# Chunk 0 halted after eight of w_out's rows, in unsplit float32 till there, and batches 6 and 7's state @ w_in made in eight float32 tiles in the pair phase

## The chip, the cores and the metric

The kernel runs on one core of a Trainium2 chip. The time is the device time of one execution in microseconds (us); less is better. TensorE (PE) multiplies, with its weight loads shown apart (PEld), VectorE (DVE) and ScalarE (ACT) work on tiles, GpSimd (POOL) does little here, and SyncE (SP) issues nearly all the transfers (DMA). Each engine works through a queue of its own in a fixed order.

## The reference

```python
def _attn_ref(x, state):                      # x: 8, 8, 512, 64   state: 8, 8, 32, 64
    scores = scale * np.matmul(x, state.transpose(0, 1, 3, 2))
    ...                                       # softmax over the 32 slots: a
    xread = np.matmul(a, state)
    scores2 = scale * np.matmul(state, x.transpose(0, 1, 3, 2))
    ...                                       # softmax over the 512 tokens: a2
    sread = np.matmul(a2, x)
    return np.concatenate([xread, sread], axis=2)

def _moe_ref(x, w_in, w_out):                 # x: 4608 tokens x 512, w_in: 512 x 2048, w_out: 2048 x 512
    h = x @ w_in
    g = h - np.tanh(h)
    return g @ w_out
```

## The kernel before

**Work.** Each of eight batches (chunk 0 to 7, 512 tokens each) never forms its xread: since xread is a @ state, its hidden layer is a @ (state @ w_in), so the kernel first makes m = state @ w_in (256 x 2048 a batch) and multiplies by a. The `sread` rows of all batches are a ninth chunk of 256 tokens at the end. Of each chunk, `hidden(f)` makes 128 of the 2048 hidden columns (f = 0 to 15) and `output(f)` multiplies them by rows 128 f to 128 f + 127 of w_out, "row f" below, and adds them up in four PSUM banks, one for each 128 tokens.

**Precision.** TensorE takes float32 operands in two ways here. A plain float32 matmul is two records in the trace. Or both operands are split in two float32r parts, high and low (`split`: ScalarE casts, VectorE subtracts), and three float32r matmuls do the work (high by high, high by low, low by high; lines 483 to 485 in `hidden`, 530 to 532 in `add`). Before the change only the first four `hidden` of chunk 0 are plain (`mlo is None`, line 481, and line 687 of the start-up); every `add` is split.

**Weights.** w_in and w_out come in as float64. Each row or tile is loaded as 512 KB and made float32 by three VectorE instructions and one ScalarE instruction (`Weight.steps`); w_out's rows are then split (`convert_wout`, tiles `wo`), and w_in's tiles go back to DRAM as float32 (`wf`) and are multiplied with the state.

**state @ w_in.** For batches 0 and 1 `m_first_two` does it while w_in is converted: eight plain matmuls of 64 x 32 weights by 512 columns, on eight parts of the array, for each pair of tiles. For batches 2 to 7 `m_units` does it later, in sixteen units: w_in is read back and split, six matmuls (line 232) make batches 2 to 5's part, three (line 239, tile `mls`) batches 6 and 7's. The results go to DRAM (`mdram`) and come back as `mr` when a chunk needs them.

**Order.** Chunks 0 to 3 are written as steps `st = 16 * i + f`. A step converts weights (`D0["conv"]`, `D0["wo"]`), writes `hidden` two steps ahead (`LAG`), then a piece of other work from tables (`ASIDE`: attention of later batches `att2` and so on, `m_units` as `m0`), then `output(f)`. Chunks 4 to 7 are done in two pairs by `Pair`, in ticks, with fewer products (sums and differences of w_out's rows, made by `mix_rows`, stand for some of them); attention of batches 6 and 7 lies in the first pair (`SIDES`). The scheduler sorts what is written into the five queues.

Of the kernel before, what the change touches and what calls it, by code (L numbers as in the profile page):

```python
# [19 lines left out]
P = 128  # L20
# [10 lines left out]
LONE = 1  # L31
TURN = (0, 1, 3, 2)
# [3 lines left out]
def attention_ffn(ctx: ExitStack, tc: tile.TileContext, xT, xn, bd, bh, sp, sm, sl, win, wout, xout, tout, sout):  # L36
# [24 lines left out]
    AB = int('2')  # L61
# [17 lines left out]
        if b >= 2  # L79
        else None  # L80
        for b in range(B)
    ]
    wf = [dram.tile([P, 4, 512], F32, name=f"wf{q}") for q in range(NQ)]
# [70 lines left out]
    def second(q):  # L154
        if q < 2:
            return pool.tile([P, 2, 512], F32, tag="stage", name=f"mr1{q}", bufs=SB)
        return pool.tile([P, 2, 512], F32, tag="g", name=f"mr1{q}", bufs=GB)

    def m_first_two(q, p):

        k = p // 2
        if p == 0:

            m_first[q] = pool.tile([P, 2, 512], F32, tag="mr", name=f"mr0{q}", bufs=RRB)
            m_second[q] = second(q)
        if p % 2 == 0:
            return
        pss = [bank(ps_a, f"mps0{q}{p - 1 + c}") for c in range(2)]
        run = []
        for b in range(2):  # L170
            for c in (1, 0):
                for e in range(2):
# [3 lines left out]
                    with ExitStack() as behind:  # L176
                        if run:
                            behind.enter_context(tc.issue_after(run[-1]))
                            behind.enter_context(tc.high_priority())
                        made = nc.tensor.matmul(  # L180
                            pss[c][rows], sps[r, p - 1 + c, rows], wfs[q, k][r, c], start=True, stop=True
                        )
                    if not run:
                        behind_free(made)
                    run.append(made.ins)
        for c in range(2):
# [18 lines left out]
    def m_units():  # L205
# [4 lines left out]
        raw = pool.tile([P, 4, P], F32, tag="stage", name="slr", bufs=SB)  # L210
        s1 = parts("sls", [P, 2, 4, P], F32R)
        nc.sync.dma_start(raw, sl)
        split(s1[:, 0], s1[:, 1], raw)
        for q in range(NQ):
            for k in range(2):
                w = pool.tile([P, 2, 512], F32, tag="wf", name=f"w1{q}{k}", bufs=WB)
                nc.sync.dma_start(w, wf[q][:, 2 * k : 2 * k + 2])
                for c in range(2):
# [4 lines left out]
                    ps2 = bank(ps_h, f"mls{q}{p}")  # L223
# [14 lines left out]
                    for n, (x, y) in enumerate(((0, 0), (0, 1), (1, 0))):  # L238
                        nc.tensor.matmul(ps2, s1[:, x, p], t[:, y], start=(n == 0), stop=(n == 2))  # L239
                    late = pool.tile([P, 512], F32, tag="c2", name=f"sl{q}{p}", bufs=CSB)  # L240
                    nc.scalar.copy(late, ps2)
                    stage = pool.tile([P, 2, 512], F32, tag="stage", name=f"st{q}{p}", bufs=SB)
                    for e in range(2):
                        free(stage[:, e], pss[e])
# [3 lines left out]
                    for e in range(2):  # L248
                        for j in range(2):
                            rows = slice(64 * e + 32 * j, 64 * e + 32 * j + 32)  # L250
                            nc.sync.dma_start(mdram[6 + j][q][k, 2 * c + e], late[rows])
                    yield

    def load_m(b, q):
        if b < 2:
            r = (m_first, m_second)[b][q]
# [25 lines left out]
    def convert_wout(f, part):  # L282
        w = pool.tile([P, 512], F32, tag="c2", name=f"wor{f}", bufs=CSB)
        part.convert(w)
        wo[f] = big(f"wo{f}", [P, 2, DM], F32R)
        split(wo[f][:, 0], wo[f][:, 1], w)


    def attention(b, aT):
# [22 lines left out]
        def all_scores():  # L312
# [3 lines left out]
            for j in (2, 0, 3, 1):  # L316
                at = TURN[j] if b < 2 else j
# [63 lines left out]
    def state_read(b, ss):  # L381
# [40 lines left out]
        for hf in range(2):  # L422
            for k in range(4):
                for c in range(4):
                    cs = slice(32 * c, 32 * c + 32)
                    j = TURN[c] if b < 2 else c
# [12 lines left out]
        for hf in range(2):  # L439
            for j in range(4):  # L440
                h = 4 * hf + (TURN[j] if b < 2 else j)
# [8 lines left out]
    def turn_sread():  # L450
        srT = pool.tile([P, 2, 4, 256], F32R, tag="aT", name="srT", bufs=AB)
# [9 lines left out]
    class Chunk:  # L461
        def __init__(self, i):
# [3 lines left out]
            self.g = {}  # L466

# [22 lines left out]
        def finish(self, f, ps):  # L490
            i, n = self.i, self.n
            t = pool.tile([P, 512], F32, tag="t", name=f"t{i}_{f}", bufs=TB)[:, :n]
            if CL <= i < B:
# [4 lines left out]
                return  # L498
            tanhs.append((nc.scalar.activation(t, ps, AF.Tanh).ins, nc.vector.tensor_sub(t, ps, t).ins))  # L499
# [4 lines left out]
        def output(self, f):  # L504
            n = self.n // P
            if f == 0:
                self.o = [bank(ps_o, f"ops{self.i}_{t}") for t in range(n)]
# [14 lines left out]
            if f == NFF - 1:  # L522
                for t in range(n):
                    self.store(t)

        def add(self, f, t):
            g, o = self.g[f], self.o[t]
            tok = slice(t * P, t * P + P)
            w = wo[f]
            nc.tensor.matmul(o, g[:, 0, tok], w[:, 0], start=(f == 0), stop=False)  # L530
            nc.tensor.matmul(o, g[:, 0, tok], w[:, 1], start=False, stop=False)  # L531
            return nc.tensor.matmul(o, g[:, 1, tok], w[:, 0], start=False, stop=(f == NFF - 1)).ins  # L532

        def store(self, t):
            i, o = self.i, self.o[t]
            ob = pool.tile([P, DM], F32, tag="ob", name=f"ob{i}_{t}", bufs=OB)
# [41 lines left out]
    def convert_win(q, p):  # L578
# [24 lines left out]
    aTs[0] = pool.tile([P, 2, 2, 512], F32R, tag="aT", name="aT0", bufs=AB)  # L603
# [26 lines left out]
    def step(op):  # L630
# [29 lines left out]
        elif k == "A":  # L660
            ats[j] = pool.tile([P, 512], F32, tag="ob", name=f"at0{j}", bufs=OB)
# [26 lines left out]
        elif k == "X":  # L688
            t = hts[j] = pool.tile([P, 512], F32, tag="t", name=f"t0_{j}", bufs=TB)
            a = nc.scalar.activation(t, hps[j], AF.Tanh)  # L690
            d = nc.vector.tensor_sub(t, hps[j], t)
# [3 lines left out]
        elif k == "G":  # L695
# [413 lines left out]
```

## Time and profile before

| | |
|---|---|
| Median of 3 runs | 664.64 us (663.02 to 666.04) |
| The profiled execution: its time, its span | 662.42 us, 660.6 us |
| Mean granted TensorE clock | 0.992 |
| Busy in the span: PE, PEld, DVE, ACT, POOL | 96%, 75%, 73%, 59%, 4% |
| Chain that ended last: PE, DVE, DMA, issue, ACT | 77%, 14%, 4%, 3%, 2% |
| HBM traffic | 93.91 MB read, 42.47 MB written |

Busy time on PE is modelled to each matmul's end, and matmuls overlap; on other engines it is the time of their instructions. A granted clock of 1.00 is 2.4 GHz, 0.50 is 1.2 GHz, and a value between is a stretch with both.

### The profile page before, as it was taken

The page shows a single profiled execution, that of the slowest core. Times are in us where ns is not written, and L with a number is a line of the kernel's source. Part 1 is how long each engine was busy: PE and PEld are TensorE (multiplying, and loading weights), DVE is VectorE, ACT ScalarE, POOL GpSimd, SP SyncE. Part 2 cuts the span into 40 slices and gives each one's busy share as a digit, 9 for nine tenths or more (in the row PEclk, how much of TensorE's full clock was granted, in tenths as well). Part 3 has the DMA queues.
Part 4 walks back from the last instruction along what each step waited for, and adds up shares of the span by engine and source line. Part 5 has one row for each costly group of instructions (what it writes and reads, how often), then busy time and mean ns, then how long its engine had stood idle before and what let it go on. Part 6 is the DMA issues. An engine that isn't in the chain of part 4 may idle for free.

```text
span 660.6 us, 9657 instructions
## 1 busy us (share of the span) xinstructions
PE 633.5 (96%) x3482; PEld 494.4 (75%) x3482; DVE 483.8 (73%) x769; ACT 389.2 (59%) x675; POOL 27.3 (4%) x41
## 2 busy tenths in 40 slices
PE   5879989999999999999999999999999999999997
PEld 2546667677777778787878887778888888788996
DVE  5999999639457876799637886996965789754442
ACT  3768875657667666576645576355655553543532
POOL 2000000000000000000000000000000000343300
PEclk9799999999999999999999999999999999999999
DMA  9799798356787974656722436464566535899800
GB/s 314 213 357 321 268 368 275 138 185 177 223 265 223 301 221 160 193 168 220 257 97 96 143 128 209 159 197 128 160 189 190 159 128 174 291 320 356 270 23 32
DMA packets 65199, 137.01 MB, mean 207 GB/s; under 512 B 6784, under 2 KB 28544, under 8 KB 65152
## 3 DMA queue, kind: packets, MB, share of 16 engines
q1 hardware_dynamic: 62592, 128.02, 59.5%
q0 software_dynamic: 2560, 8.39, 3.7%
q8 instruction: 27, 0.44, 0.3%
q14 instruction: 20, 0.16, 0.1%
HBM read 93.91 MB, written 42.47 MB: 206 GB/s over the span
## 4 chain that ended last, share of the span: by engine, by line
PE 77%; DVE 14%; DMA 4%; issue 3%; ACT 2%; SPq 0%; ACTq 0%; DVEq 0%
PE X L944 12%; PE hps L483 9%; PE hps L484 8%; PE hps L485 8%; PE ops L532 8%; PE ops L531 8%; PE ops L530 8%; PE Y1m L944 5%; PE Y0m L944 4%; PE mps L232 2%; PE mls L239 2%; PE rps L431 1%; DVE m L101 1%; DMA wo3d<-in_wout 1%; DVE w L131 1%
## 5 line engine op out<-in xcount | busy, mean ns | idle before, releaser
L531 PE MATMUL ops<-wo,g 128*128 128x512 f32 x256 | 99.9, 394 | 6.0 <-DVE wo L101 6.0
L483 PE MATMUL hps<-aT,m 128*128 128x512 f32 x248 | 99.3, 402 | 3.3 <-DVE G L497 1.3
L484 PE MATMUL hps<-aT,m 128*128 128x512 f32 x248 | 97.0, 391 | 0.0
L485 PE MATMUL hps<-aT,m 128*128 128x512 f32 x248 | 96.3, 391 | 0.0
L530 PE MATMUL ops<-wo,g 128*128 128x512 f32 x256 | 94.1, 396 | 0.9 <-ACT wo L101 0.8
L532 PE MATMUL ops<-wo,g 128*128 128x512 f32 x256 | 90.5, 394 | 0.0
L499 DVE TENSOR_TENSOR t<-hps,t 128x512 f32<-128x512 f32 (+1 forms) x78 | 49.5, 634 | 51.6 <-ACT t L499 51.3
L497 ACT ACTIVATE t<-hps 128x512 f32<-128x512 f32 x64 | 38.3, 599 | 61.8 <-PE hps L485 59.5
L497 DVE TENSOR_TENSOR G<-hps,t 128x512 f32<-128x512 f32 x64 | 43.9, 688 | 36.9 <-ACT t L497 36.9
L499 ACT ACTIVATE t<-hps 128x512 f32<-128x512 f32 (+1 forms) x78 | 43.3, 555 | 44.9 <-PE hps L485 42.3
L101 ACT CAST g<-t 128x512 fp32r<-128x512 f32 (+1 forms) x78 | 44.8, 579 | 32.0 <-DVE t L499 31.8
L483 PEld LDWEIGHTS hps<-aT,m 128*128 128x128 f32 x248 | 46.4, 188 | 22.9 <-ACT m L101 3.6
L531 PEld LDWEIGHTS ops<-wo,g 128*128 128x128 f32 x256 | 48.2, 188 | 19.0 <-DVE wo L101 8.3
L101 DVE TENSOR_TENSOR g<-t,g 128x512 fp32r<-128x512 f32 (+1 forms) x78 | 49.2, 633 | 14.8 <-ACT g L101 14.4
L530 PEld LDWEIGHTS ops<-wo,g 128*128 128x128 f32 x256 | 47.7, 188 | 16.4 <-ACT wo L101 3.0
L532 PEld LDWEIGHTS ops<-wo,g 128*128 128x128 f32 x256 | 48.2, 189 | 11.1 <-issue 0.8
L485 PEld LDWEIGHTS hps<-aT,m 128*128 128x128 f32 x248 | 46.5, 188 | 10.3 <-DVE m L101 0.4
L484 PEld LDWEIGHTS hps<-aT,m 128*128 128x128 f32 x248 | 46.6, 188 | 8.9
L982 POOL DMA_DIRECT2D wl<-wod x32 | 23.4, 730 | 590.9 <-DVE g1m L101 556.4
L944 PE MATMUL X<-g0m,W0m 128*128 128x512 f32 x192 | 46.9, 390 | 0.5 <-DVE g0m L101 0.5
L944 PE MATMUL X<-g1m,W1m 128*128 128x512 f32 x192 | 45.9, 391 | 0.6 <-DVE g1m L101 0.6
L101 ACT CAST g1m<-G 128x1024 fp32r<-128x1024 f32 x28 | 29.2, 1054 | 28.9 <-PE Y1m L944 12.7
(257 smaller groups left out, 1128.2 us busy)
## 6 DMA issues: line engine op xcount, KB each, us to landing
mr<-md SPq DMA_DIRECT2D x24, 512.0 KB, 3.8
xT<-in_xT SPq DMA_DIRECT2D x16, 512.0 KB, 4.9
wod<-wo SPq DMA_DIRECT2D x32, 256.0 KB, 6.1
md<-st SPq DMA_DIRECT2D x64, 128.0 KB, 2.4
xn<-in_xn SPq DMA_DIRECT2D x16, 512.0 KB, 5.3
wsd<-ws SPq DMA_DIRECT2D x16, 512.0 KB, 4.8
W0m<-wsd SPq DMA_DIRECT2D x16, 512.0 KB, 4.0
W1m<-wsd SPq DMA_DIRECT2D x16, 512.0 KB, 4.5
```

Of the source, the lines that this page charges most:

```text
L101: return nc.scalar.copy(hi, src), (sub or nc.vector).tensor_sub(lo, src, hi)
L232: made = nc.tensor.matmul(pss[e], s0[rows, x, 2 * p + e], t[rows, y], start=(n == 0), stop=(n == 2))
L483: nc.tensor.matmul(ps, mhi[k][:, cols], ahi[:, k], start=(k == 0), stop=False)
L484: nc.tensor.matmul(ps, mhi[k][:, cols], alo[:, k], start=False, stop=False)
L485: made = nc.tensor.matmul(ps, mlo[k][:, cols], ahi[:, k], start=False, stop=(k == nk - 1))
L497: main(nc.scalar.activation(t, ps, AF.Tanh), nc.vector.tensor_sub(g, ps, t))
L499: tanhs.append((nc.scalar.activation(t, ps, AF.Tanh).ins, nc.vector.tensor_sub(t, ps, t).ins))
L530: nc.tensor.matmul(o, g[:, 0, tok], w[:, 0], start=(f == 0), stop=False)
L531: nc.tensor.matmul(o, g[:, 0, tok], w[:, 1], start=False, stop=False)
L532: return nc.tensor.matmul(o, g[:, 1, tok], w[:, 0], start=False, stop=(f == NFF - 1)).ins
L944: made = nc.tensor.matmul(out[t], w[:, e, x, cols], y[:, e], start=first and j == 0 and e == 0 and c == 0, stop=last and j == 3 and e == 1 ...
L982: nc.gpsimd.dma_start(wo[f][:, :, cols].bitcast(F32), wod[:, f % 2, half, f // 2])
```

## The change

- Chunk 0's first eight rows of w_out are kept as plain float32 (`plain`, tiles `wp`), and `hidden` 0 to 7 and `output` 0 to 7 of chunk 0 are plain float32 too: g is not split there. `split_row` splits those rows afterwards, at steps 6 to 13.
- After row 7 chunk 0 halts (`HALT`): its four sums go to DRAM (`halfd`), chunk 1 runs all its sixteen steps, then chunk 0 does rows 8 to 15 in a second set of sums, to which the first is added (`load_partial`).
- Weights are converted later and thinner: w_in's third and fourth quarter and w_out's rows 8 to 15 fall into chunk 1's steps. m of batch 0's third and fourth quarter goes to DRAM and back. Attention of batch 1 moves to steps 0 to 5, the split of chunk 0's own a (`split_first`) from the start-up to step 18.
- `m_units` no longer makes batches 6 and 7; `m_last_two` does, in eight units of eight plain matmuls as in `m_first_two`, at ticks 0 to 32 of the first pair, with w_in read back once more.

```diff
+HALT = 8
+PLAIN = 8
...
+    def eight(name, held, w):
+        pss = [bank(ps_a, f"mps{name}{c}") for c in range(2)]
...
+                        made = nc.tensor.matmul(pss[c][rows], held(c, r, rows), w[r, c], start=True, stop=True)
...
+        if q >= 2 and k:
+            nc.sync.dma_start(mdram[0][q].rearrange("g h n f -> (h n) g f"), m_first[q])
...
-                    for n, (x, y) in enumerate(((0, 0), (0, 1), (1, 0))):
-                        nc.tensor.matmul(ps2, s1[:, x, p], t[:, y], start=(n == 0), stop=(n == 2))
-                    late = pool.tile([P, 512], F32, tag="c2", name=f"sl{q}{p}", bufs=CSB)
-                    nc.scalar.copy(late, ps2)
...
+    def m_last_two():
...
+        for n, (q, k) in enumerate(units):
+            w = following
+            pss = eight(f"l{q}{k}", lambda c, r, rows: spl[r, 2 * k + c, rows.start // 64], w)
+            stage = pool.tile([P, 2, 512], F32, tag="stage", name=f"sl{q}{k}", bufs=SB)
+            for c in range(2):
+                free(stage[:, c ^ 1], pss[c ^ 1])
+            for b in range(2):
+                for c in range(2):
+                    dst = mdram[6 + b][q][k, 2 * c : 2 * c + 2]
+                    nc.sync.dma_start(dst.rearrange("h n f -> (h n) f"), stage[64 * b : 64 * b + 64, c])
...
     def convert_wout(f, part):
+        if f < PLAIN:
+            if f % 2 == 0:
+                plain[f // 2] = big(f"wp{f}", [P, 2, DM], F32)
+            part.convert(plain[f // 2][:, f % 2])
+            return
...
+    def split_row(f):
+        wo[f] = big(f"wo{f}", [P, 2, DM], F32R)
+        split(wo[f][:, 0], wo[f][:, 1], plain[f // 2][:, f % 2])
...
+            if i == 0 and f < PLAIN:
+                g = self.g[f] = pool.tile([P, 512], F32, tag="g", name=f"g{i}_{f}", bufs=GB)
+                tanhs.append((nc.scalar.activation(t, ps, AF.Tanh).ins, nc.vector.tensor_sub(g, ps, t).ins))
+                return
...
+        if self.i == 0 and f < PLAIN:
+            w = plain[f // 2][:, f % 2]
+            return nc.tensor.matmul(o, g[:, tok], w, start=(f in self.begins), stop=stop).ins
...
+    def load_partial(self):
+        for t in range(self.n // P):
+            p = pool.tile([P, DM], F32, tag="c2", name=f"part{t}", bufs=CSB)
+            nc.sync.dma_start(p, halfd[t])
...
+        if self.partial:
+            nc.vector.tensor_add(ob, o, self.partial[t])
...
+    WO = [0, 1, 2, 3, 4, 5, 6, 8, 9, 10, 12, 13, 14, 15, 16]
+    SPLITS = [6 + x for x in range(PLAIN)]
...
-        "att1": D0["att"]["1"],
+        "att1": [0, 1, 2, 3, 4, 5],
+        "first": [18],
...
+            "m6": [0, 4, 8, 12, 16, 19, 23, 29, 32],
...
+    order = [(0, f) for f in range(HALT)] + [(1, f) for f in range(NFF)] + [(0, f) for f in range(HALT, NFF)]
+    order += [(i, f) for i in range(2, CL) for f in range(NFF)]
+    for st, (i, f) in enumerate(order):
```

How the queues change is shown at three places. A row names line, operation, output and inputs; `x2` is two in a row.

PE's queue before, from chunk 0's first output on (`ops0_t` are the four sums, `wo0` row 0, `g0_0` the hidden columns, `mps01` of `m_first_two`):

```order
L530 MATMUL ops0_0_340<-wo0_275,g0_0_226 128x512
L530 MATMUL ops0_1_341<-wo0_275,g0_0_226 128x512
L530 MATMUL ops0_2_342<-wo0_275,g0_0_226 128x512
L530 MATMUL ops0_3_343<-wo0_275,g0_0_226 128x512
L481 MATMUL hps0_3_375<-at00_185,mr00_131 128x512
L481 MATMUL hps0_3_375<-at01_206,mr00_131 128x512
L180 MATMUL mps011_299<-w010_280,sps_111 32x512 x2
L180 MATMUL mps010_298<-w010_280,sps_111 32x512 x2
L180 MATMUL mps011_299<-w010_280,sps_111 32x512 x2
L180 MATMUL mps010_298<-w010_280,sps_111 32x512 x2
L531 MATMUL ops0_0_340<-wo0_275,g0_0_226 128x512
L532 MATMUL ops0_0_340<-wo0_275,g0_0_226 128x512
```

The same place in the changed kernel's PE queue (`wp0` holds rows 0 and 1 unsplit):

```order
L569 MATMUL ops0_0_0_343<-wp0_266,g0_0_230 128x512
L569 MATMUL ops0_0_1_344<-wp0_266,g0_0_230 128x512
L569 MATMUL ops0_0_2_345<-wp0_266,g0_0_230 128x512
L569 MATMUL ops0_0_3_346<-wp0_266,g0_0_230 128x512
L173 MATMUL mps0101_293<-w010_274,sps_116 32x512 x2
L514 MATMUL hps0_3_359<-at00_190,mr00_136 128x512
L514 MATMUL hps0_3_359<-at01_211,mr00_136 128x512
L173 MATMUL mps0100_292<-w010_274,sps_116 32x512 x2
L173 MATMUL mps0101_293<-w010_274,sps_116 32x512 x2
L173 MATMUL mps0100_292<-w010_274,sps_116 32x512 x2
L569 MATMUL ops0_0_0_343<-wp0_266,g0_1_234 128x512
```

Where row 0 took twelve matmuls, eight of which waited for the split's low part, it takes four plain ones that read the row as soon as it is converted.

DVE's queue before, where attention of batch 1 begins (`e10`, `e11`), while chunk 0 is at its ninth and tenth step:

```order
L499 TENSOR_TENSOR t0_8_706<-hps0_8_699,t0_8_706 128x512
L130 TENSOR_SCALAR wor9_806<-wo9d_617 128x512
L101 TENSOR_TENSOR wo7_691<-wor7_685,wo7_691 128x512
L134 ISA wor8_732<-wor8_732,wo8r_733 128x1024
L499 TENSOR_TENSOR t0_9_750<-hps0_9_743,t0_9_750 128x512
L131 SCALAR_TENSOR_TENSOR wor9_806<-wo9d_617,wor9_806 128x512
L130 TENSOR_SCALAR wor10_817<-wo10d_683 128x512
L101 TENSOR_TENSOR wo8_738<-wor8_732,wo8_738 128x512
L348 STREAM_TRANSPOSE e10_659<-s1_656 128x512
```

The changed kernel's DVE queue where that attention begins now (`g0_4` is the fifth hidden column of chunk 0, `wo0` the split of row 0):

```order
L136 ISA wp6_482<-wp6_482,wo7r_501 128x1024
L534 TENSOR_TENSOR g0_4_414<-hps0_4_410,t0_4_413 128x512
L534 TENSOR_TENSOR g0_5_439<-hps0_5_435,t0_5_438 128x512
L103 TENSOR_TENSOR wo0_524<-wp0_266,wo0_524 128x512
L379 STREAM_TRANSPOSE e10_393<-s1_390 128x512
L379 STREAM_TRANSPOSE e11_417<-s1_390 128x512
L381 TENSOR_REDUCE m110_395<-e10_393 128x16
L381 TENSOR_REDUCE m111_419<-e11_417 128x16
L534 TENSOR_TENSOR g0_6_466<-hps0_6_462,t0_6_465 128x512
```

The last conversion of chunk 0's first eight rows now stands ahead of `g0_4`, no g is split, and the attention stands behind `g0_4` and `g0_5`, four steps earlier than before.

ACT's queue in the first pair before, from `hidden(12)` of chunk 4 on:

```order
L497 ACTIVATE t4_12_3884<-hps4_12_3877 128x512
L391 ACTIVATE s60_3682,rs60_3892<-s60_3682,nm60_3890 128x512
L497 ACTIVATE t4_13_3910<-hps4_13_3903 128x512
L497 ACTIVATE t4_14_3921<-hps4_14_3914 128x512
L101 CAST g0m130_3973<-G4_12_3885 128x1024
```

The same place now (`mpsl` are the two banks of one unit of `m_last_two`, `sl` the staging tile that four transfers then empty):

```order
L530 ACTIVATE t4_12_3693<-hps4_12_3686 128x512
L422 ACTIVATE s60_3449,rs60_3701<-s60_3449,nm60_3699 128x512
L203 COPY sl10_3743<-mpsl101_3734 128x512
L203 COPY sl10_3743<-mpsl100_3733 128x512
L530 ACTIVATE t4_13_3719<-hps4_13_3712 128x512
L530 ACTIVATE t4_14_3730<-hps4_14_3723 128x512
L103 CAST g0m130_3801<-G4_12_3694 128x1024
```

Two copies of each unit stand between the tanhs of chunk 4 and 5, and they wait for the unit's matmuls and for the staging tile.

## Rows read from the trace of the kernel before

**Rows 1.** The page's first part: busy time, share of the span, number of instructions.

```profile
PE 633.5 (96%) x3482; PEld 494.4 (75%) x3482; DVE 483.8 (73%) x769; ACT 389.2 (59%) x675; POOL 27.3 (4%) x41
```

**Rows 2.** Windows, of 20 us first and then by stage: start and end, length, busy time (and instructions) of PE, PEld, DVE, ACT, POOL, granted clock, share of the DMA engines, GB/s.

```profile
20.00:40.00 20.00, 17.39 (x72) 10.44 (x71) 18.39 (x34) 17.28 (x35) 0.00 (x0) 0.90 0.78 232
40.00:60.00 20.00, 15.90 (x84) 9.99 (x83) 18.70 (x35) 14.08 (x25) 0.00 (x0) 0.91 1.00 363
60.00:80.00 20.00, 18.89 (x114) 12.46 (x114) 18.95 (x35) 18.40 (x33) 0.00 (x0) 1.00 0.79 270
80.00:100.00 20.00, 18.25 (x88) 13.02 (x87) 20.00 (x37) 14.74 (x26) 0.00 (x0) 1.00 1.05 367
...
29.78:119.35 89.57, 79.82 (x398) 53.80 (x396) 82.94 (x148) 65.21 (x113) 0.00 (x0) 0.97 0.90 311
119.35:140.00 20.65, 20.65 (x94) 15.45 (x95) 11.77 (x17) 13.25 (x24) 0.00 (x0) 1.00 0.45 141
140.00:405.00 265.00, 264.88 (x1671) 206.44 (x1670) 193.86 (x350) 170.93 (x319) 0.00 (x0) 1.00 0.60 193
405.00:450.00 45.00, 42.72 (x196) 33.22 (x195) 40.88 (x43) 22.47 (x34) 0.00 (x0) 1.00 0.57 178
```

**Rows 3.** The waits of PE from 20 to 125 us: who waited for whom, us in total, times, longest.

```profile
PE ops L531 <- DVE wo L101: 6.0, 5, 2.5
PE mps L679 <- DVE w L134: 2.4, 1, 2.4
PE hps L483 <- DVE t L499: 1.0, 1, 1.0
```

**Rows 4.** PE's groups by line and shape from 20 to 119.4 us: count, busy time and mean ns, idle time before.

```profile
L531 PE MATMUL ops<-wo,g 128*128 128x512 f32 x64 | 25.2, 408 | 6.0 <-DVE wo L101 6.0
L532 PE MATMUL ops<-wo,g 128*128 128x512 f32 x64 | 24.2, 398 | 0.0
L530 PE MATMUL ops<-wo,g 128*128 128x512 f32 x64 | 18.7, 406 | 0.9 <-ACT wo L101 0.8
L483 PE MATMUL hps<-aT,m 128*128 128x512 f32 x29 | 11.5, 409 | 1.9 <-DVE t L499 1.0 <-ACT m L101 0.8
L484 PE MATMUL hps<-aT,m 128*128 128x512 f32 x28 | 11.0, 391 | 0.0
L485 PE MATMUL hps<-aT,m 128*128 128x512 f32 x28 | 10.5, 393 | 0.0
L180 PE MATMUL mps<-w,sps 64*32 64x512 f32 x96 | 7.2, 659 | 1.1 <-ACT mr L197 1.1
L481 PE MATMUL hps<-at,mr 128*128 128x512 f32 x8 | 4.3, 666 | 0.0
```

**Rows 5.** The chain that ended last, in order of time: start, length, what. Here a group's length is the time it took of the chain.

```profile
144.14 1.02 PE sps L324 x16
145.16 0.43 PE hps L483
145.58 0.23 PE hps L484
...
479.93 2.72 PE Y0m L944 x12
```

**Rows 6.** The timeline of PE and PEld: start, length, engine, line, what, idle time before and its releaser. The first two are weight loads of plain matmuls that follow one another; then the first plain `hidden` behind the start-up, and the last wait of the start.

```profile
33.40 0.19 PEld L481 LDWEIGHTS hps<-at,mr 128*128 128x128 f32 x1 [0.24 <-issue]
33.83 0.19 PEld L481 LDWEIGHTS hps<-at,mr 128*128 128x128 f32 x1 [0.24 <-issue]
...
29.78 2.43 PE L481 MATMUL hps<-at,mr 128*128 128x512 f32 x4
...
119.35 0.50 PE L483 MATMUL hps<-aT,m 128*128 128x512 f32 x1 [0.96 <-DVE t L499]
```

**Rows 7.** The timeline of DVE, same columns: five instructions that follow one another without a wait, from 52.57 us, and the one that takes chunk 0's first hidden column.

```profile
22.77 0.68 DVE L691 TENSOR_TENSOR t<-hps,t 128x512 f32<-128x512 f32 x1
...
52.57 1.22 DVE L101 TENSOR_TENSOR m<-mr,m 128x1024 fp32r<-128x1024 f32 x1
53.70 0.69 DVE L101 TENSOR_TENSOR wo<-wor,wo 128x512 fp32r<-128x512 f32 x1
54.30 0.69 DVE L134 CUSTOM_DVE_ANT_0 wor<-wor,wo4r 128x1024 uint16<-128x1024 uint16 x1
54.91 0.43 DVE L130 TENSOR_SCALAR w<-w30d 128x512 uint32<-128x512 uint32 x1
55.24 0.42 DVE L130 TENSOR_SCALAR w<-w31d 128x512 uint32<-128x512 uint32 x1
```

**Rows 8.** Windows of 4 us, columns as in rows 2.

```profile
44.00:48.00 4.00, 1.54 (x7) 0.93 (x6) 4.00 (x8) 1.11 (x2) 0.00 (x0) 0.99 1.04 419
48.00:52.00 4.00, 3.53 (x21) 1.11 (x19) 4.00 (x10) 3.93 (x7) 0.00 (x0) 0.58 0.94 337
```

**Rows 9.** The waits of PE and of ACT, columns as in rows 3: PE's from 125 us to the end, then ACT's from 400 to 450 us.

```profile
PE hps L483 <- DVE G L497: 1.3, 2, 1.1
...
ACT t L497 <- PE hps L485: 11.1, 9, 2.0
```

**Rows 10.** What is replaced: PE's group of line 239, by shape; and the page's transfers of the units' results, KB each, us from issue to landing.

```profile
L239 PE MATMUL mls<-wst,sls 128*128 128x512 f32 x48 | 14.5, 409 | 0.0
...
md<-st SPq DMA_DIRECT2D x64, 128.0 KB, 2.4
```

More of the change, by code (lines that the diff above doesn't have):

```diff
@@ L82, in attention_ffn @@
     ]
+    halfd = dram.tile([4, P, DM], F32, name="halfd")
     wf = [dram.tile([P, 4, 512], F32, name=f"wf{q}") for q in range(NQ)]
@@ L154, in second @@
     def second(q):
[L155 to L168, printed above, removed]
+        return pool.tile([P, 2, 512], F32, tag="stage", name=f"mr1{q}", bufs=SB)
+    def eight(name, held, w):
+        pss = [bank(ps_a, f"mps{name}{c}") for c in range(2)]
         run = []
@@ L185, in m_first_two @@
                     run.append(made.ins)
+        return pss
+    def m_first_two(q, p):
+        k = p // 2
+        if p == 0:
+            tag, bufs = ("m", MB) if q == 1 else ("mr", RRB)
+            m_first[q] = pool.tile([P, 2, 512], F32, tag=tag, name=f"mr0{q}", bufs=bufs)
+            m_second[q] = second(q)
+        if p % 2 == 0:
+            return
+        pss = eight(f"0{q}{k}", lambda c, r, rows: sps[r, p - 1 + c, rows], wfs[q, k])
         for c in range(2):
@@ L247, in m_units, with held_w @@
                         nc.sync.dma_start(dst.rearrange("h n f -> n h f"), stage[32 * j : 32 * j + 32])
[L248 to L251, printed above, removed]
                     yield
+    def m_last_two():
+        def held_w(q, k):
+            w = pool.tile([P, 2, 512], F32, tag="wf", name=f"w2{q}{k}", bufs=WB)
+            nc.sync.dma_start(w, wf[q][:, 2 * k : 2 * k + 2])
+            return w
+        spl = pool.tile([P, 4, 2, NS], F32, tag="x", name="spl", bufs=XB)
+        nc.sync.dma_start(spl, sl)
+        units = [(q, k) for q in range(NQ) for k in range(2)]
+        following = held_w(*units[0])
+        yield
+        for n, (q, k) in enumerate(units):
[8 more added lines that the diff above has]
+                    nc.sync.dma_start(dst.rearrange("h n f -> (h n) f"), stage[64 * b : 64 * b + 64, c])
+            if n < 7:
+                following = held_w(*units[n + 1])
+            yield
     def load_m(b, q):
-        if b < 2:
-            r = (m_first, m_second)[b][q]
+        if b == 0 and q < 2:
+            return [m_first[q][:, k] for k in range(2)], None
+        if b == 1:
+            r = m_second[q]
         else:
@@ L466, in __init__ @@
             self.g = {}
+            self.begins = (0, HALT) if i == 0 else (0,)
+            self.partial = []
         def prepare(self, q):
@@ L721, in attention_ffn @@
     a0 = state_read(0, ss)
-    split_first()
     late1 = late_read(1)
@@ L838, in attention_ffn @@
                     load(1)
-            nf = f + LAG
-            if nf < NFF:
+            if st + LAG < len(order):
+                ni, nf = order[st + LAG]
                 if nf % 4 == 0:
-                    chunks[i].prepare(nf // 4)
-                chunks[i].hidden(nf)
-            elif i < CL - 1:
-                if nf == NFF:
-                    chunks[i + 1].prepare(0)
-                chunks[i + 1].hidden(nf - NFF)
+                    chunks[ni].prepare(nf // 4)
+                chunks[ni].hidden(nf)
+            with ExitStack() as gates:
+                for x in tanhs[max(st - 1, 0)]:
+                    gates.enter_context(tc.issue_after(x))
+                for _ in range(SPLITS.count(st)):
+                    split_row(next(split_it))
             if st in AHEAD:
@@ L853, in attention_ffn @@
                 chunks[i + 1].reached = x
-            for _ in range(D0["pair"].count(st)):
+            for _ in range(PAIRS.count(st)):
                 m_first_two(*next(pairs))
```

125 lines of the change are left out of this document (48 added, 77 removed).

## The prediction

> **What bounds the kernel now.** The page's first part comes first: PE is busy 96% of the span, no other engine over 75% [rows 1]. The windows then show where PE is not full [rows 2]: from 119.35 us to the end it idles only from 405 to 450 us (42.72 of 45.00 busy). From 29.78 us, where the first plain `hidden` behind the start-up begins, to 119.35 us, where PE's last wait of the start ends [rows 6], PE is busy 79.82 of 89.57 us, and DVE works 18.39 to 20.00 of each 20 us: there DVE, converting weights, sets the time. PE's waits name it: 6.0 us for `wo`, 2.4 us for `w`, 1.0 us for a tanh's subtraction [rows 3].
>
> How much of those 89.57 us could come back is counted by slots, the time after which the next instruction of a kind starts. Twelve float32r matmuls take 2.72 us, 0.2267 each; sixteen records of eight small ones take 1.02, and the matmul behind them 0.43 where the next takes 0.23, so an "eight" costs 1.22 [rows 5]. The records of plain matmuls follow each other 0.43 us apart (0.427, twice the 0.2135 of 512 columns at 2.4 GHz) [rows 6]. In this stretch stand 192 matmuls of `add` and 85 of `hidden`, 8 records of plain `hidden`, 96 records of `m_first_two` (six eights) and one eight of scores [rows 4]. Less the matmul that starts as the stretch ends, that is 276 x 0.2267 + 8 x 0.427 + 7 x 1.22 = 62.6 + 3.4 + 8.5 = 74.5 us of work. **So 15.1 us are lost there.** 9.75 us of it is idle in the row; some 2.7 is the clock, granted 0.97 of full speed over the stretch: after PE had idled in 44 to 48 us it was granted 0.58, partly 1.2 GHz [rows 8]; the rest is hidden by modelled ends.
>
> The Trainium skill (Perfetto Trace Analysis, Identifying the Most-Contended Engine) says that matmul busy time is no good measure of how close TensorE is to its limit, and that the busy share of weight loads is a better one. By the busy row 9.75 us could be won, by weight loads (53.80 us here, against 206.44 in 265.00 where PE is full [rows 2]) 89.57 - 69.1 = 20.5. With the first the sum below would end at 0.9 us less than before, with the second at 11.6 less; I keep the count by slots, which lies between.
>
> **The change, part by part.**
>
> *Plain float32.* Of chunk 0's rows 0 to 7, 32 outputs (eight by four) take two records, 0.854 us, in place of three matmuls, 0.680: +0.174 each, +5.6. `hidden` 4 to 7 are two products each, eight in all: +1.4. **+7.0 on PE.** DVE loses the eight g subtractions (0.60 each by the starts of [rows 7], 4.8 us) and shifts the eight splits of rows behind the first outputs; those do not vanish.
>
> *Batches 6 and 7.* The 48 matmuls of line 239 [rows 10] go from a stretch in which PE is full: -48 x 0.2267 = -10.9. Eight eights come into the pair phase: +8 x 1.22 = +9.8. **-1.1.** The sixteen copies that emptied their banks become sixteen copies of the staging tiles, so ACT's work is moved, not grown.
>
> *The start-up's stalls.* I add slots along the queues. DVE after, from g0_0 to its last instruction before g0_4: 42 instructions, of which 12 shifts (0.335, by the starts 54.91 and 55.24), one subtraction of 128x1024 (1.13), 29 others (0.60) [rows 7] = 22.6 us, so from about 22.4 to 45. PE from f2 on needs for f2 to f5, output(0) to output(3) and two eights: 4 x 1.71 + 4 x 3.42 + 2 x 1.02 = 22.6 us, from about 28.8 to 51.4. PE has taken the lead that DVE had; DVE is some 6 us early for g0_4, which is the cover for a late weight (if it goes, every us over 6 is lost). Then scores of batch 1, f6, f7, output(4) to (7) and one eight are 19 us on PE, to 70.5; the attention chain, 35 DVE instructions or 18.9 us from 53.6, gives chunk 1's a at 72.5: **2 us of wait**. From there to f11 of chunk 1 DVE has 82 instructions, 47.5 us, and PE 12 x 1.36 + 10 x 2.72 + 3 x 1.22 + 0.9 = 48: level. Behind that DVE's 39.5 us stand against 44 on PE, so PE leads to the end of the conversion. A level stretch leaves waits where single items come late: before, DVE itself idled in 20 to 100 us though it set the pace, 80 - 76.0 = 4 us [rows 2]; I take 3 us of it for PE. So 15.1 us of loss become 5: **-10.1**. Bounds: 1.5 (half a microsecond at three handovers) to 15 (nothing gained, DVE stays the pace): -13.6 to 0.
>
> *Start of f2.* The two subtractions of chunk 0's a and two of its g stood on DVE and their casts on ACT about PE's wait of 2.4 us [rows 3]; I take **-1.0**, between 0 and three subtractions of 0.60, -1.8.
>
> *The halt.* Four sums go out and come back (1 MB each way) and chunk 1's first output waits for their banks. Two copies each on ACT and DVE of about 0.6 us are covered by `hidden` of two steps ahead (2 x 1.36): 0; without that cover +1.2. On SP the stores of the halt stand ahead of seven weight loads and would hold them by the wait for the copies (at about 71 to 73 us); DVE wants those weights from about 90 on: 0. The partial sum is added where a copy was: 0.
>
> *Pair phase.* PE now stands still 2.3 us of 405 to 450 [rows 2], with single waits of 1.3 us for DVE's G [rows 9]; eights that come there take time in which DVE catches up. They are in PE's queue ahead of what waits, so some of the 2.3 us is filled with work already counted: **-1.0**, between 0 and -2.3. ACT waits 11.1 of 50 us for PE's `hidden` there [rows 9], so the copies have room. Each unit reads 512 KB of w_in again and stores 512 KB; 8.4 MB over some 52 us adds 160 GB/s to 178 at a DMA share of 0.57 [rows 2]; the start ran at 363 to 367 GB/s at a share of about 1.0. So DMA comes near its limit, and landings get longer than the 2.4 us that the units' stores take now [rows 10]; the tile is asked for again two units (13 us) later, which hides that.
>
> **Sum:** +7.0 - 1.1 - 10.1 - 1.0 - 1.0 = -6.2. The profiled execution took 662.42 us (span 660.6 and 1.8 around it), 2.2 under the median of 664.64. After: 656.2 by the profile's own time, **658.4 us for the median**.
>
> **Rivals.**
>
> *All of the start-up's waits go.* Stalls fall to 1.5 and f2 and the pair phase give their bounds: +7.0 - 1.1 - 13.6 - 1.8 - 2.3 = -11.8, 652.8. For it: DVE's 6 us lead at g0_4. Against: the level stretch in chunk 1.
>
> *DVE keeps the pace of the start-up.* Items in the in-order queue (a late weight, the attention chain) still take 10 us from PE: -1.2, so 663.4. For it: DVE was full at 80 to 100 us [rows 2], and nearly the same conversions must be done. Against: the slots, by which PE's own work to f11 of chunk 1 is as long as DVE's.
>
> *Slower: ACT held in the pair phase.* A unit's two copies wait for its staging tile, in line ahead of chunk 4 and 5's tanhs. If DMA near its limit makes the four stores of a unit land late, every tanh behind waits, and PE with it. Each microsecond a unit is held costs up to 8; against the -6.2 it makes the kernel measurably slower from 9.5 us, 1.2 us in each unit. Held by one landing of 2.4 us in six units: +14.4, so 672.8. For it: the added 160 GB/s. Against: 13 us between uses of one tile, and PE's lead in `hidden`.
>
> *The plain products cost more than 0.174 each beyond their slots* (a refill at every change between plain and split, 0.2 as behind an eight): 16 changes, +3.2, so 661.6; it goes into the range.
>
> **How the numbers follow.** The forecast (654 to 661.3, stalls of 1 to 8 us) has 0.5. All waits gone has 0.15, DVE keeping the pace 0.22, the slower rival 0.13. The likeliest gives 658.4. 0.5% of 664.64 is 3.3 us, about what a measurement here can tell from no change: faster is below 661.3, slower above 668.0. Faster takes the forecast, all waits gone and a small part of the third, 0.68; same the most of the third and mild holds of ACT, 0.20; slower 0.12. The range leaves out the slower rival's full price and under one in ten below: 651.5 (all waits gone, 652.8, and most of its last 1.5 us of stalls) to 666.
>
> **What will show it.** Right: 64 records of line 569 at 0.43 us; PE idle from 29 to 120 us under 5 us, with one wait of about 2 us at chunk 1's first `hidden`; granted clock near 1.00 at 44 to 52 us; eights of line 173 at 1.02 us in the pair phase, PE's waits there under 1.5 us. The halt is right if `ops1` waits less than 1 us. Wrong: PE's waits for `wo` and `w` staying near 9 us, a wait for `wp` over the 6 us lead, or ACT's copies of `sl` waiting for SP's transfers. Most in doubt is the level stretch of chunk 1: an error of a tenth in DVE's 47.5 us is 4.7 us.

## The result, and the profile after

The changed kernel takes 669.75 us (median of 6 runs, 668.08 to 671.42) where the kernel before took 663.97 in runs beside it: 1.0091 times as long, 95% interval 1.0071 to 1.0110. It was forecast at 658.4, between 651.5 and 666.0. Its profiled execution has a span of 666.3 us, 5.7 more than the one of before.

First the stages, as in [rows 2]: start and end, length, busy time (and instructions) of PE, PEld, DVE, ACT, POOL, granted clock, DMA share, GB/s. The first stretch begins with the first plain `hidden` behind the start-up; the last is the pair phase.

```profile
28.32:80.29 51.97, 47.64 (x164) 19.09 (x165) 39.46 (x72) 29.93 (x53) 0.00 (x0) 1.00 0.72 249
80.29:166.59 86.30, 82.63 (x412) 61.41 (x412) 74.63 (x131) 61.42 (x109) 0.00 (x0) 1.00 0.88 293
166.59:261.50 94.91, 92.06 (x544) 69.49 (x544) 63.09 (x114) 53.93 (x101) 0.00 (x0) 0.98 0.64 197
405.00:450.00 45.00, 45.00 (x300) 32.98 (x299) 40.56 (x43) 25.18 (x41) 0.00 (x0) 1.00 0.76 261
```

The start-up is what the prediction wanted: PE waits only 4.3 us up to 80.29 us and is full behind that to 162 us, at full clock. The pair phase, 42.72 of 45.00 us busy before [rows 2], has no idle left. But PE is idle in the two stretches between, where it was full before. PE's timeline shows each wait after 28 us of over half a microsecond up to 300 us (start, length, line, idle time before and its releaser):

```profile
45.44 1.13 PE L514 MATMUL hps<-at,mr 128*128 128x512 f32 x2 [0.74 <-ACT mr L203]
76.69 0.73 PE L516 MATMUL hps<-aT,m 128*128 128x512 f32 x2 [1.91 <-ACT aT L103]
80.29 0.50 PE L516 MATMUL hps<-aT,m 128*128 128x512 f32 x1 [1.61 <-DVE t L536]
166.59 0.50 PE L571 MATMUL ops<-wo,g 128*128 128x512 f32 x1 [3.68 <-DVE ob L595]
261.54 0.50 PE L516 MATMUL hps<-aT,m 128*128 128x512 f32 x1 [2.89 <-ACT m L103]
```

The last two are new: 3.68 us for a bank of chunk 1's sums, and 2.89 us for a tile of batch 2's m. Of the waits of [rows 3], those for `wo` are gone.

**The account.** Weight loads are complete in both traces (3482 and 3522, one for each matmul). I took the gap between the starts of each two that follow one another, and against it the usual gap of such a pair (0.2267 us between float32r matmuls, 0.429 between plain records, and so on); what is over is waiting or half clock. The usual gaps are a little long between 120 and 300 us, where the kernel before comes out below zero; the difference is what counts. In us:

| | before | after | difference | forecast |
|---|---|---|---|---|
| first load of f2 | 29.4 | 28.3 | -1.0 | -1.0 |
| work behind it | 612.4 | 621.8 | +9.4 | +5.9 |
| lost to 120 us | 14.2 | 3.5 | -10.7 | -10.1 |
| lost 120 to 300 us (against the usual gaps) | -2.2 | 7.7 | +9.9 | 0 |
| lost 300 to 455 us | 3.2 | 1.2 | -2.0 | -1.0 |

The sum is +5.6. Three lines came at or near the forecast; two did not. The loss between 120 and 300 us is what most of the experiments are about.

**Where the waits come from.** The sixteen units of `m_units` slipped behind the `hidden` and `output` written around them, the last ones furthest. The weight loads of all units, before and after (number, shortest/median/longest ns, first and last start):

```profile
L232 PEld LDWEIGHTS mps<-wst,sms x96: 182/185/186, 124.1 to 235.9; 64*128 64x128 f32 x96
```

```profile
L233 PEld LDWEIGHTS mps<-wst,sms x96: 182/185/186, 122.4 to 249.5; 64*128 64x128 f32 x96
```

In PE's queue the last unit stood behind output(4) of chunk 2 before, and stands behind output(9) now, though the table still asks for the same step, 34, the third of chunk 2: that is five steps later than before and seven later than the table. It makes the last quarter of batch 2's m, which chunk 2's `hidden` 12 wants. The chain (start, length, what) shows its way through DRAM, behind SP's queue, while PE has nothing left that it may do:

```profile
254.48 0.60 ACT p2t L203
...
255.21 5.21 DMA mr<-md
...
260.44 1.04 ACT m L103
```

The wait at 162 us has the same root. SP's queue issues in order, and at 148 us eight stores of two units stand in it one behind the other. The last row is ScalarE's copy that brings the second unit's results:

```profile
148.10 8.16 SPq L244 DMA_DIRECT2D md<-st  x8
156.36 0.38 SPq L219 DMA_DIRECT2D w<-wf  x1
156.84 0.39 SPq L279 DMA_DIRECT2D mr<-md  x1
157.32 1.73 SPq L599 DMA_DIRECT2D out_x<-ob  x2
160.13 1.77 SPq L837 DMA_DIRECT2D wsd<-ws  x2
...
153.44 1.07 ACT L203 COPY st<-mps 128x512 f32<-128x512 f32 x2
```

Of the 8.16 us SP waits 4.7, between the fourth store and the fifth, which starts at 154.53 us; it had also waited 3.7 us ahead of the row. Then everything behind it goes out close together. The windows of 4 us show the hole, the burst that follows, and the clock behind PE's wait:

```profile
152.00:156.00 4.00, 4.00 (x21) 3.05 (x21) 4.00 (x8) 3.10 (x7) 0.00 (x0) 1.00 0.17 39
...
164.00:168.00 4.00, 1.41 (x6) 1.19 (x7) 2.15 (x4) 2.25 (x4) 0.00 (x0) 0.98 1.08 394
168.00:172.00 4.00, 4.00 (x13) 3.09 (x12) 3.75 (x9) 3.21 (x7) 0.00 (x0) 0.59 0.31 119
```

39 GB/s, then, 8 us later, 394. Chunk 1's stores, issued in this stretch, take 4.5 to 7.8 us to land, the two `ob` buffers are not free, the third and fourth sum keep their banks, and chunk 0's second half can't begin. PE idles 3.68 us and is then granted 0.59 in 168 to 172 us.

### The profile page after: what moved, and what is told of

It is laid out like the page before. It is cut to its first block, busy times and chain, and to the rows that moved or that the text cites. A ratio compares the mean times of both kernels' runs of the same rounds, so it can differ in the third digit from the quotient of the medians.

```text
span 666.3 us, 9704 instructions
## 1 busy us (share of the span) xinstructions
PE 638.4 (96%) x3522; PEld 479.3 (72%) x3522; DVE 480.7 (72%) x763; ACT 382.6 (57%) x665; POOL 27.2 (4%) x41
## 4 chain that ended last, share of the span: by engine, by line
PE 82%; DVE 6%; DMA 6%; ACT 4%; issue 1%; SPq 0%; ACTq 0%; DVEq 0%
PE X L980 13%; PE hps L516 9%; PE hps L517 9%; PE hps L518 9%; PE ops L571 8%; PE ops L572 8%; PE ops L573 8%; PE Y0m L980 5%; PE Y1m L980 5%; PE mps L233 2%; DMA out_x<-ob 1%; PE mpsl L173 1%; DMA wo3d<-in_wout 1%; DMA w01d<-in_win 1%; PE rps L462 1%
## 5 line engine op out<-in xcount | busy, mean ns | idle before, releaser
L516 PE MATMUL hps<-aT,m 128*128 128x512 f32 x240 | 96.7, 405 | 9.1 <-ACT m L103 2.9
L517 PE MATMUL hps<-aT,m 128*128 128x512 f32 x240 | 94.1, 392 | 0.1
L518 PE MATMUL hps<-aT,m 128*128 128x512 f32 x240 | 93.3, 391 | 0.0
L571 PE MATMUL ops<-wo,g 128*128 128x512 f32 x224 | 87.9, 397 | 3.7 <-DVE ob L595 3.7
L572 PE MATMUL ops<-wo,g 128*128 128x512 f32 x224 | 88.1, 395 | 0.0
L573 PE MATMUL ops<-wo,g 128*128 128x512 f32 x224 | 80.3, 395 | 0.0
L536 DVE TENSOR_TENSOR t<-hps,t 128x512 f32<-128x512 f32 (+1 forms) x72 | 45.1, 626 | 31.4 <-ACT t L536 31.1
L516 PEld LDWEIGHTS hps<-aT,m 128*128 128x128 f32 x240 | 44.9, 188 | 31.3 <-DVE G L530 5.6
L536 ACT ACTIVATE t<-hps 128x512 f32<-128x512 f32 (+1 forms) x72 | 39.6, 551 | 37.3 <-PE hps L518 35.2
L103 ACT CAST g<-t 128x512 fp32r<-128x512 f32 (+1 forms) x72 | 41.0, 573 | 32.0 <-DVE t L536 31.8
L103 DVE TENSOR_TENSOR g<-t,g 128x512 fp32r<-128x512 f32 (+1 forms) x72 | 45.1, 627 | 13.6 <-ACT g L103 13.3
L571 PEld LDWEIGHTS ops<-wo,g 128*128 128x128 f32 x224 | 42.1, 189 | 16.5 <-DVE ob L595 4.1
L517 PEld LDWEIGHTS hps<-aT,m 128*128 128x128 f32 x240 | 45.2, 188 | 10.2 <-issue 1.1
L518 PEld LDWEIGHTS hps<-aT,m 128*128 128x128 f32 x240 | 45.1, 188 | 10.1 <-DVE m L103 0.5
L572 PEld LDWEIGHTS ops<-wo,g 128*128 128x128 f32 x224 | 42.3, 189 | 10.9 <-issue 2.3
L573 PEld LDWEIGHTS ops<-wo,g 128*128 128x128 f32 x224 | 41.9, 189 | 10.3 <-DVE t L536 0.8
```

What stands on the lines that cost most here:

```text
L103: return nc.scalar.copy(hi, src), (sub or nc.vector).tensor_sub(lo, src, hi)
L516: nc.tensor.matmul(ps, mhi[k][:, cols], ahi[:, k], start=(k == 0), stop=False)
L517: nc.tensor.matmul(ps, mhi[k][:, cols], alo[:, k], start=False, stop=False)
L518: made = nc.tensor.matmul(ps, mlo[k][:, cols], ahi[:, k], start=False, stop=(k == nk - 1))
L571: nc.tensor.matmul(o, g[:, 0, tok], w[:, 0], start=(f in self.begins), stop=False)
```

## The experiments

Each kernel is the changed one but for the edit shown, unless it says otherwise; ratios are against the kernel before, run beside it (664.27, 665.04 and 664.22 us in the three sets).

**e1: four store buffers.**

```diff
-    OB = int('2')
-    GB = int('7')
+    OB = int('4')
+    GB = int('6')
```

> Four buffers instead of two for the sums on their way out (ob), and six instead of seven for g to make room; nothing else. In the changed kernel PE waits 3.7 us at 162 us for a bank of chunk 1's sums, whose copy waits for a store's landing (7.0 us), and is granted half clock for 3.4 us behind it (1.7 us lost). Theory (waits given back behind the start-up): the wait and the half clock go, 5.4 us less than the changed kernel, about 664.4 us by a changed kernel of 669.75. Rival (the transfers themselves are the limit there, the buffers only show it): the wait comes back at the next load, under 1.5 us less, 668.5 or more.

663.43 us, ratio 0.9976 (0.9953 to 0.9999): 6.3 less than the changed kernel. The landing is no shorter, but nothing waits for it (under neither heading of the view is there a line):

```profile
its engine sat idle before it (us, times) until:
who waited for it (us, times):
...
DMA to landing us min/median/max: 7.5/7.7/7.8
```

PE is full from 156 to 172 us at clock 1.00, and waits 2.07 us for m near 254 us as before. So that wait and its half clock were real losses and not the transfers' own limit.

**e3: the part on batches 6 and 7 alone, in the kernel before.**

```diff
-                    ps2 = bank(ps_h, f"mls{q}{p}")
...
-                        nc.tensor.matmul(ps2, s1[:, x, p], t[:, y], start=(n == 0), stop=(n == 2))
...
+    def m_last_two():
...
+            "m6": [0, 4, 8, 12, 16, 19, 23, 29, 32],
```

In this kernel and in e4, two heads of each four of batches 6 and 7 are exchanged between m and a; the work is the same.

> The kernel before with one part of the change alone: batches 6 and 7's state @ w_in in eight plain units in the first pair instead of three matmuls in each of the sixteen units. By the prediction's step: -1.1 us of PE work and -1.0 in the pair, 662 us where before is 664. Theory: an eight among float32r matmuls costs 1.35 us, not 1.22, so the work is level (8 x 1.35 = 10.8 against 10.9), and without the three matmuls, whose bank stands in line with those of hidden, the sixteen units slip behind by up to seven steps, so that chunk 2's hidden 12 waits for the last unit's round trip through DRAM: 2.9 us and half clock, 666 to 668 us, with PE waiting for m near chunk 2's output(11).

667.02 us, ratio 1.0047 (1.0023 to 1.0071): slower than before by this part alone. Work behind f2 is 612.6 us against 612.4, level. The units slip as in the changed kernel, and PE waits where it waited there (units' loads; PE's wait for m):

```profile
L227 PEld LDWEIGHTS mps<-wst,sms x96: 182/185/186, 124.9 to 248.9; 64*128 64x128 f32 x96
```

```profile
259.86 0.63 PE L515 MATMUL hps<-aT,m 128*128 128x512 f32 x1 [1.95 <-ACT m L101]
```

Between 240 and 300 us it loses some 5 us against before. Halt and plain rows are not needed for that. The wait for a store buffer at 162 us does not come here: without the halt no chunk ends there.

**e4: that part undone in the changed kernel**, with the three matmuls of line 239 back in each unit.

> The changed kernel with the part on batches 6 and 7 undone: three matmuls in each of the sixteen units again, no eights in the pair. Theory: the last unit stands behind chunk 2's output(4) again and the wait of 2.9 us at 258 us and the half clock about it go; the pair's own waits come back (2 us): 1.5 to 3.5 us less than the changed kernel, 666.2 to 668.2 us. The prediction's steps: 2.1 us more, 671.9 us.

669.29 us, ratio 1.0077 (1.0047 to 1.0106): no measurable gain; both were wrong. The units end at 240.7 us and the wait for m is gone. So is the one at 162 us: the fourth unit runs on PE at the same time as in the changed kernel (149.6 and 149.4 us), but ScalarE copies its sums at 150.35 us and not at 153.44, and chunk 1's stores land in 2.1 to 2.8 us (the copy; landing of `ob`):

```profile
150.35 1.08 ACT L203 COPY st<-mps 128x512 f32<-128x512 f32 x2 [1.46 <-DMA md<-st]
DMA to landing us min/median/max: 2.1/2.3/2.8
```

But PE waits elsewhere:

```profile
216.15 0.50 PE L584 MATMUL ops<-wo,g 128*128 128x512 f32 x1 [2.25 <-DVE ob L604]
433.27 0.50 PE L529 MATMUL hps<-aT,m 128*128 128x512 f32 x1 [1.09 <-DVE G L543]
```

The store buffers are short at chunk 0's end now, and the pair's waits of [rows 9] are back. Why just there was not followed.

**e5: the units held in step.** No work is changed; one order is added.

```diff
+                    unit[0] = run[-1]
...
-                chunks[ni].hidden(nf)
+                with ExitStack() as pin:
+                    if unit[0] is not None:
+                        pin.enter_context(tc.issue_after(unit[0]))
+                    chunks[ni].hidden(nf)
```

> The changed kernel with one rule more: hidden of a step is ordered behind the last matmul of the unit written a step before it, so that the units can't slip; same work. Theory: the wait for m at 258 us goes, 3 to 4 us less than the changed kernel, 666 to 667 us; the wait for the store buffers at 162 us stays. Rival (the slip is harmless, and the wait is of another cause, such as DMA): within 1 us of the changed kernel.

662.16 us, ratio 0.9968 (0.9956 to 0.9980): 7.6 less than the changed kernel, and faster than the kernel before. More than expected, because the wait for the store buffers went too. The pin costs something of its own: PE now waits 1.8 us near 141 us, where a unit's banks wait for ScalarE's copies. The units end at 220.4 us; SP's hole is filled, and the stores of chunk 1 land in under half the time (units' loads; the same window as above; landing of `ob`):

```profile
L235 PEld LDWEIGHTS mps<-wst,sms x96: 182/185/187, 123.6 to 220.4; 64*128 64x128 f32 x96
```

```profile
152.00:156.00 4.00, 4.00 (x20) 2.80 (x19) 3.97 (x9) 2.89 (x6) 0.00 (x0) 1.00 0.82 225
```

```profile
DMA to landing us min/median/max: 2.7/2.8/3.1
```

**e11: the crowd in the burst thinned**, by moving the row sums and their 1 MB stores behind chunk 1.

```diff
-    MIX = [24, 28, 32, 36, 40, 44, 48, 52]
+    MIX = [33, 35, 37, 39, 42, 45, 48, 52]
```

> The changed kernel, with the sums and differences of w_out's rows and their stores (1 MB each time) moved from steps 24, 28, 32, 36, ... to 33, 35, 37, 39, ..., past the end of chunk 1; two store buffers as it has. Asks why a store of 256 KB takes 7.0 us at 158 us: if the crowd of other transfers (1 MB of sums, 512 KB each of a tile of w_in and of m, 512 KB of a unit) is the cause, the landing falls under 5 us and the wait for the bank from 3.7 to 1.5 or less, 2.5 to 5 us less than the changed kernel. Rival (in-order issue on the queue): the landing stays and the time is within 1.5 us.

668.02 us, ratio 1.0048 (1.0025 to 1.0072). By landing and wait the rival is right. The two stores that hold the banks land in 7.8 and 7.9 us (the 2.1 in the row is of the two later ones), and PE waits 3.5 us (landing; PE's waits). The time, 1.7 us less than the changed kernel by the medians, lies between theory and rival.

```profile
DMA to landing us min/median/max: 2.1/4.9/7.9
```

```profile
PE ops L571 <- ACT ob L593: 3.5, 1, 3.5
```

SP again spent 8.13 us on eight stores of two units. So it is not the sums that make the landing long. That it is the other transfers held up behind SP's wait, of which two reads of 512 KB are issued just ahead of the stores, is argued and was not tried.

**e6: pin and four buffers together.**

> The units pinned as in the run that orders hidden behind them, and four store buffers, together. Alone they took 7.6 and 6.3 us off the changed kernel's 669.75. Theory (two causes, each with its own wait, and the pin also moves chunk 1's stores out of the crowded stretch): little more than the pin alone, 0.5 to 2.5 us less than its 662.16: 659.7 to 661.7 us. If the two were separate in full, 656; if they were one and the same wait, 662.

663.21 us, ratio 0.9962 (0.9945 to 0.9979): no more than the pin alone: what four buffers gave, the pin had already given.

**e8: e3 with the pin**, both heads in their place.

> The kernel before with batches 6 and 7 made in the pair and the units pinned, without halt and without plain rows beyond those it had. Theory: the part on batches 6 and 7 is level in work, and the slip of the units is its only loss; pinned, the waits at 240 to 270 us go (4 to 5 us) and the pair's waits (1.3 and 0.5 us) stay filled: 1 to 3.5 us less than before, 660.8 to 663.3 us. Rival (the eights themselves cost, by DMA traffic or by ScalarE in the pair): 665 us or more.

665.72 us, ratio 1.0019 (1.0002 to 1.0036). In part a miss: the loss of 240 to 300 us is gone (some 5 us), but the pin brought waits of its own (PE 2.6 us for ScalarE at a unit, 2.0 for `ob`), so the part on batches 6 and 7 gains nothing in the old order even when pinned.

**e7 and e9: fewer plain rows**, on e6 (`PLAIN = 4` and `PLAIN = 2`).

> The same with rows 4 to 7 split at once, as before the change, and only rows 0 to 3 plain. PE has 16 outputs less in plain float32, 16 x 0.174 = 2.8 us less work; VectorE gets four subtractions of g and has four of rows to do before chunk 0's fifth to eighth output, 4.8 us, in a stretch (28 to 80 us) in which it was busy 39.5 of 52 us. Theory (the plain products' price on PE is what is left of the loss): 2 to 3 us less than with eight plain rows. Rival (vector-bound start): PE waits for wo again, no gain or up to 2 us more.

> Only rows 0 and 1 plain, 24 outputs less in plain float32: 24 x 0.174 = 4.2 us less PE work than with eight plain rows, and six subtractions of g and of rows each, 7.2 us more on VectorE ahead of chunk 1. Theory: with 12 us of VectorE idle there, 3 to 4 us less than with eight plain rows. Rival (the subtractions stand in the way of the weights of the next rows): the waits for wo come back, more than with four plain rows.

668.63 us, ratio 1.0066 (1.0040 to 1.0091), and 663.30, ratio 0.9975 (0.9954 to 0.9997). The price of plain products was right: work behind f2 falls from 621.9 us to 619.0 and 617.5, 0.18 us for each of the 16 and 24 outputs, where 0.174 was put down. But nothing was won, since waits come back (e7):

```profile
PE hps L519 <- ACT aT L103: 4.5, 1, 4.5
PE mps L235 <- ACT st L203: 3.5, 1, 3.5
PE hps L517 <- ACT mr L203: 2.2, 1, 2.2
```

Not `wo`, as the rival had it: what is late is chunk 1's a and chunk 0's second tile of m, and a unit. From f2 to 80 us e7 and e9 lose 7.9 us each where e6 loses 3.3. VectorE's idle time there was no room to put work into. For e7 this is not the whole: its median is 5.4 us above e6's, but the profiled executions, the fastest of e7 and the slowest of e6, are only 0.7 us apart, so the rest is not explained.

**e10 and e12: attention of batch 1 earlier**, on e5 (`"att1": [0, 0, 1, 2, 3, 4]`), e12 with `PLAIN = 2` as well.

> The pinned units, and the attention of batch 1 one step earlier from its second piece on (steps 0, 0, 1, 2, 3, 4). In the pinned kernel some 6 us are lost between 60 and 100 us, behind the wait for chunk 1's a (1.9 us in the changed kernel) and for the tanh next to it (1.6 us). Theory (the attention chain is late, not VectorE full: it is idle 12.5 of 52 us there): 2.5 to 4 us less than the pinned kernel's 662.16, 658.2 to 659.7 us. Rival (the chain takes VectorE's time from the weights, which then are late): within 1 us of it.

> As the run with attention of batch 1 earlier and the units pinned, and rows 2 to 7 split at once, so that only rows 0 and 1 are plain: 3.6 us less PE work by the slots of the run with two plain rows. Theory: with chunk 1's a no longer late, that work is a gain in full but for a late weight, 2 to 3.6 us less than the same with eight plain rows. Rival (VectorE's 7.2 us more stand in the attention chain's way): no gain, or up to 3 us more.

666.43 us, ratio 1.0031 (1.0007 to 1.0056), and 663.63, ratio 0.9981 (0.9962 to 1.0001). e10 takes 4.3 us more than the pin alone, which neither theory nor rival had. e12 takes 2.8 us less than e10, within the theory's range, but it is not faster than the pin alone. The waits are of the rivals' kind. In e10 nothing is lost any more between 60 and 100 us, but chunk 0's later columns wait (3.2 us for g, 1.9 for m's tile) between 40 and 60 us, and in e12 a piece of `m_first_two` waits 5.7 us for the scores:

```profile
PE mps L173 <- ACT s L203: 5.7, 1, 5.7
```

## Why the prediction was wrong

**Right.** The plain products (+7.0; e7 and e9 give 0.18 an output). The start-up's stalls: 15.1 to 5 us was the forecast; by the loads it is 14.2 to 3.5. By the Trainium skill's rule on weight loads' busy share (Perfetto Trace Analysis, Identifying the Most-Contended Engine) 20.5 us stood to be won there, by busy time 9.75; the count by slots was the nearest to the 14.2 that were lost. The start of f2 (-1.0), and the pair phase (-2.0 where -1.0 was taken): the slower rival, ScalarE held there, did not come, PE is full from 405 to 450 us.

**Right by luck: the wait of 2 us for chunk 1's a.** It came, with 1.9 us, but not from the attention chain. PE was to reach chunk 1's `hidden` at 70.5 us; it reached it at 73.1 and stopped at 74.8 for the second half of a. DVE had written a's last transpose at 73.4 us, and what was late was the cast on ACT, behind the copy of a sum that waited for a store of the halt:

```profile
75.53 0.58 ACT L593 COPY ob<-ops 128x512 f32<-128x512 f32 x1 [4.34 <-DMA halfd<-ob]
76.02 0.62 ACT L103 CAST aT<-at 128x512 fp32r<-128x512 f32 x1
```

With four buffers (e1) ACT does not wait there, and PE still waits 1.6 us, because the cast then stands behind four copies of `mr`.

**The step that failed first: what is moved off a stretch was costed as PE time alone.** "The 48 matmuls of line 239 [rows 10] go from a stretch in which PE is full: -48 x 0.2267 = -10.9." So they do. But the bank of their sums came from the pool of `hidden`'s two banks, so a unit could not fall behind the `hidden` written after it. Without it nothing held the units, and in the order the last one slipped to seven steps behind its place in the table. The order was to be seen before the run; the prediction read it at the start-up and the pair and not between. It put nothing down for 120 to 300 us; 9.9 us were lost there. That the slip is the cause of the wait for m is shown by e3, which has it without halt or plain rows, and by e5, which takes it away without changing work. For the wait at 162 us, e1 shows that the store buffers make it, and e4 and e5 that it goes when the units are held; it takes the halt as well, which puts chunk 1's end there. That it is the bank that held them is argued from the code: a copy and four stores went out of each unit with it, and were not tried apart.

**The halt's step** ("two copies each on ACT and DVE ... 0, without that cover +1.2") named the right thing, banks that wait to be copied out, and the wrong cover. It looked at copies of 0.6 us; what held the banks is the store behind the copy (7 us, two buffers), which was priced for batches 6 and 7's tiles but not for `ob`. It was also sought at chunk 0's halt, where the stores of 70.7 to 76.9 us cost PE little (1.9 us of waiting for a, 1.6 with four buffers), and came at chunk 1's end.

**The term that was mis-sized: work, +9.4 for +5.9.** An eight was priced at 1.22 us from the chain [rows 5], which begins with the eight and so leaves out what stands ahead of it. The weight loads of the changed kernel (start, length; idle before) show both sides:

```profile
32.29 0.19 PEld L569 LDWEIGHTS ops<-wp,g 128*128 128x128 f32 x1 [0.24 <-issue]
32.72 0.19 PEld L569 LDWEIGHTS ops<-wp,g 128*128 128x128 f32 x1 [0.24 <-issue]
33.66 0.14 PEld L173 LDWEIGHTS mps<-w,sps 64*32 64x32 f32 x4 [0.76 <-issue]
34.64 0.30 PEld L514 LDWEIGHTS hps<-at,mr 128*128 128x128 f32 x2 [0.84 <-ACT t L534]
...
36.56 0.17 PEld L173 LDWEIGHTS mps<-w,sps 64*32 64x32 f32 x12 [0.76 <-issue]
37.56 0.30 PEld L569 LDWEIGHTS ops<-wp,g 128*128 128x128 f32 x2 [0.84 <-DVE wp L132]
```

0.94 us from the last plain load to the eight where 0.43 is usual, and 0.98 from the eight to the next: 1.5 us among plain matmuls. Among float32r the two gaps are 0.54 and 0.94; with 0.08 for the eight's own loads and less the 0.23 that the matmul ahead takes anyway, that is 1.33 us. So 8 x 1.33 = 10.6 all but cancels the 10.9 that line 239 took, as e3's level work shows. The other 2 us lie in the start-up, as the rows show: one eight is cut in two by `hidden` 3 (4 and 12 of its loads above), as the order quoted ahead of the prediction already had it, and pays twice; and eights now stand between plain records.

**The rivals.** The one on the other side was put in the pair phase, where nothing was lost; the loss came some 150 to 240 us earlier, from what the same edit took out of the units.

## What to carry to other kernels

Work that is taken out of a queue takes its constraints with it: before a removal is booked as time saved, ask which shared buffer or bank kept the remaining work in step, and read the new order from the place of the removal to the next consumer. A unit that stores to DRAM through an in-order queue and slips can delay what stands behind it twice, by the hole and by the crowd after it; a rule of order that costs no work (e5) was worth at least as much here as more buffers (e1). Price a switch of matmul shape from the last ordinary weight load ahead of it to the first behind it, less their usual gap.

## What the runs showed of the hardware

A wait of 3.5 to 3.7 us on PE was followed by half clock (granted 0.59 in 168 to 172 us, 0.50 in e11), one of 2.89 us at 261 us by none (1.00 from 257 to 266 us); in e3 two waits of 0.72 and 1.95 us, 3 us apart, were followed by it again (0.57 in 260 to 264 us). The length of one wait did not tell which. A 256 KB store landed in 2.7 to 3.1 us with the queue fed at 225 to 300 GB/s (e5), and in 7.0 to 7.9 us where it was issued right behind SP's wait and two reads of 512 KB (the changed kernel's first two, e1, e11). It did so with 327 and 394 GB/s moved in 160 to 168 us (the changed kernel) and with 263 and 236 (e11), so the rate alone did not set it.
